# A routed attention and feed-forward kernel: when the first weight pieces are asked for and made up, and the order of factor stores and factor fetches

## The chip, the cores and the metric

The kernel runs on one core of one Trainium2 chip. Its time is the device time of one execution in microseconds. Three runs of the kernel before gave 940.28, 940.62 and 939.73, median 940.28. A profile is one more execution, taken by the hardware profiler: it took 940.7, of which the profile's span, from the first to the last instruction, is 938.8.

## The reference

Attention in which a query sees only the keys that were assigned to the same centroid, followed by a feed-forward block with the activation h - tanh(h). There are 4 batches, 8 heads, 768 positions of 64 elements, 16 centroids per head, and weights of 512 x 2048 and 2048 x 512 that come as 64-bit floats.

```python
q_assign = np.argmax(np.einsum('bhsd,hcd->bhsc', q_n, c_n), axis=-1)
k_assign = np.argmax(np.einsum('bhsd,hcd->bhsc', k_n, c_n), axis=-1)
mask = q_assign[:, :, :, None] == k_assign[:, :, None, :]
scores = scale * np.matmul(q, k.transpose(0, 1, 3, 2))
scores = np.where(mask, scores, -1000000000.0)
...
attn = attn / (np.sum(attn, axis=-1, keepdims=True) + 1e-09)
attn_out = np.matmul(attn, v)
...
h = x @ w_in
g = h - np.tanh(h)
return (g @ w_out)
```

## The kernel before

**Pairs, halves, steps.** Two heads are handled together, so there are 16 pairs, four to a batch. A pair's queries come in two halves of 384. The list `steps` holds (pair, half, s): each step takes two blocks of 128 keys (`s` is 0, 1 or 2) against one half of queries. Steps 0 to 11 are the first halves of the pairs of batch 0, 12 to 23 their second halves; from step 24 on a pair runs both halves in a row. `HALF` is 12. The loop over steps emits the program of all engines in a fixed order, written out by hand: nothing is moved by a scheduler afterwards, so an instruction waits behind whatever was emitted before it on its engine.

**One step.** `begin` of the next step computes scores on TensorE (L508, with a mask by one-hot codes added at L519 for pairs 1 to 3 of the first halves) and the exponential on ScalarE (L530). `value` multiplies the weights of this step with `vals` (L565). Where the mask is not in the scores, VectorE masks the weights with the codes of the queries, spread over all partitions in a tile `row` (`select`, L540). The tile pool for scores has two buffers, so the scores of one step want the exponentials of the step before.

**Codes.** The assigned centroid of each position is its code. `route` and `route_on` find it, `publish` (L439 to L443) puts the codes into `listed_codes` as a VectorE copy, transposes them and stores them to HBM in the tensor `q_codes`; `spread` (`row`) and `spread_both` (`hot`) read them back so that each partition has them all. `turn` makes the transposed tiles of queries and keys; for the first pairs it does so on TensorE, and copies the result out of PSUM on the engine that it is given (L369), or half and half on two engines if it is given none (L371, L372). `turn(0, 1, None)` stands in `centroid_norms`.

**Weight pieces.** The weights arrive as 32 pieces of 512 KB, 64-bit words that must be made into 32-bit ones. `fetch(at)` asks for a piece from POOL's queue (L218) into one of three buffers `raw`; `rest_of` makes a partial result on ScalarE (L150, L151) into one of two buffers `rest`; `round_piece` finishes it on VectorE (L159, L162) and fetches the piece three further on. The dictionary `paces` says how many pieces are made up in each of the steps 0 to 20. The first three fetches stand in the prologue, each behind a gate: `held_back(x)` is a POOL copy of one column that waits until `x` is there (L1304).

**Factors.** The later batches multiply with a scheme that needs seven combinations of quarters of each weight matrix instead of eight products of quarters. `up_maker` and `down_maker` compute the combinations on VectorE (`made`, L848; up to three live at a time) and store them, and the plain quarters that are needed as they are, to HBM (L831, from SP's queue); `maker` makes the list of such items. The items of `down_maker` are emitted in the steps 36 and 38 to 41, with a share of the list in each. From there the tiles are streamed: `fetch_factors` (L871) and `fetch_extra` (L1017) load them into the freed quarters of `w_in`. `EXTRAS_AT` says in which steps the first three extra factors (products 6, 7 and 4 of the half batch that is still open) are fetched. All SP loads and stores leave from one queue, in the order of emission.

Of the kernel before, what the change touches and what calls it, by code (L numbers as in the profile page):

```python
# [58 lines left out]
def kernel(  # L59
# [10 lines left out]
    nc = tc.nc  # L70
# [12 lines left out]
    TB = S // 2  # L83
# [25 lines left out]
    listed_codes = const.tile([P, 32], BF16, name="listed_codes")  # L109
# [70 lines left out]
    def fast():  # L180
# [29 lines left out]
        def fetch(at: int):  # L210
            if at >= len(PIECES):
                return
            dst, src = PIECES[at]
            if words == 1:
                nc.gpsimd.dma_start(dst, src)
                return
            raws[at] = rawp.tile([P, 2 * FQ * P], U32, name="raw")
            nc.gpsimd.dma_start(raws[at], src)  # L218
# [30 lines left out]
        def late_constants():  # L249
            nc.vector.tensor_scalar_mul(out=cn, in0=cen, scalar1=rden)  # L250
            spread_ = const.tile([P, 2, D], F32, name="spread_")
            nc.vector.memset(spread_, 0.0)
            nc.vector.tensor_copy(
                out=spread_[:, :, 0:C], in_=down.unsqueeze(1).to_broadcast([P, 2, C])
            )
            spread_ = spread_.rearrange("p a c -> p (a c)")
            nc.vector.tensor_tensor(out=spread_, in0=spread_, in1=ident, op=ALU.mult)
            nc.vector.reduce_sum(out=mine_code, in_=spread_, axis=AX.X)
# [9 lines left out]
        def centroid_norms():  # L268


            sq = const.tile([P, D], F32, name="sq")
            ss = const.tile([P, 1], F32, name="ss")
            nc.vector.tensor_tensor(out=sq, in0=cen, in1=cen, op=ALU.mult)
            nc.vector.reduce_sum(out=ss, in_=sq, axis=AX.X)
            nrm = const.tile([P, 1], F32, name="nrm")
            nc.scalar.sqrt(nrm, ss)

            nc.scalar.activation(out=sq[0:1, 0:1], in_=nrm[0:1], func=ACT.Exp)

            for it in range(2):  # L280
                lim = const.tile([P, 1], F32, name=f"lim{it}")
                nc.vector.tensor_scalar_max(lim, nrm, TINY)
                rec = const.tile([P, 1], F32, name=f"rec{it}")
                nc.vector.reciprocal(out=rec, in_=lim)
                two = const.tile([P, 1], F32, name=f"two{it}")
                nc.vector.scalar_tensor_tensor(
                    out=two, in0=ss, scalar=rec, in1=nrm, op0=ALU.mult, op1=ALU.add
                )
                nrm = const.tile([P, 1], F32, name=f"nrm{it}")
                nc.vector.tensor_scalar_mul(out=nrm, in0=two, scalar1=0.5)  # L290
            den = const.tile([P, 1], F32, name="den")
            nc.vector.tensor_scalar_add(den, nrm, 1e-6)
            nc.vector.reciprocal(out=rden, in_=den)
            both = const.tile([P, 2, D], F32, name="both")
            nc.vector.scalar_tensor_tensor(
                out=both, in0=cen.unsqueeze(1).to_broadcast([P, 2, D]), scalar=rden,
                in1=mines.unsqueeze(2).to_broadcast([P, 2, D]), op0=ALU.mult, op1=ALU.mult,
            )
            turn(0, 0, nc.scalar)
            pc = ps_a.tile([P, P], F32, name="pc", tag="a")  # L300
            nc.tensor.transpose(out=pc, in_=both.rearrange("p a d -> p (a d)"), identity=ident)
            nc.vector.tensor_copy(out=bd.rearrange("p a c -> p (a c)"), in_=pc)
            turn(0, 1, None)

        def keep_warm(times: int):

# [42 lines left out]
        def turn(n: int, i: int, engine):  # L349

            if not rowwise(n):
                x = raw_qk.pop((n, i))
                pool = turnp0 if n in (2, 3) else turnp
                t = turned[n, i] = pool.tile([P, 2, TB], F32, name=f"t{i}")
                nc.vector.transpose(
                    out=t.rearrange("p a n -> p (a n)"), in_=x.rearrange("p b d -> p (b d)")
                )
                return
            pt = ps_s.tile([P, 2, 512], F32, name="pt", tag="s")
            x = raw_qk.pop((n, i))  # L360
            for j in range(NCH):
                nc.tensor.transpose(
                    out=pt[:, j // HCH, (j % HCH) * P : (j % HCH + 1) * P],
                    in_=x[:, j].rearrange("p h d -> p (h d)"), identity=ident,
                )
            pool = turnp0 if n in (2, 3) else turnp
            t = turned[n, i] = pool.tile([P, 2, TB], F32, name=f"t{i}")
            if engine is nc.scalar:
                nc.scalar.copy(out=t, in_=pt[:, :, 0:TB])  # L369
                return  # L370
            nc.scalar.copy(out=t[:, 0], in_=pt[:, 0, 0:TB])  # L371
            nc.vector.tensor_copy(out=t[:, 1], in_=pt[:, 1, 0:TB])  # L372

        sims = {}

# [57 lines left out]
        def publish(n: int):  # L433

            sides = 2 if masked(n, 0) else 1
            G = HCH * 4 * sides
            code = codes[n] if sides == 2 else codes[n][:, 0]
            code = code.rearrange("p a b c -> p (a b c)" if sides == 2 else "p j h -> p (j h)")
            nc.vector.tensor_copy(out=listed_codes[:, 0:G], in_=code)  # L439
            t = rtp.tile([P, BL], BF16, name="qc")  # L440
            nc.vector.transpose(out=t, in_=listed_codes)
            kept = dram.tile([BL, P], BF16, name="q_codes")
            nc.sync.dma_start(kept.rearrange("c (g t) -> g c t", t=BL), t)  # L443
            if sides == 1:
                q_codes[n] = kept[0:G].rearrange("(a j h) p -> a j h p", a=2, h=2)
            else:
                q_codes[n] = kept[0:G].rearrange("(h i a j) p -> h i a j p", h=2, i=sides, a=2)

        rows, hots = {}, {}
# [392 lines left out]
        def maker(quarters, their, sums_, keep, shape, last=False):  # L842
            made = {}

            def make(which, x, y, op):
                x, y = (made[i] if isinstance(i, int) else i for i in (x, y))
                t = made[which] = rawp.tile(shape, F32, name="made", tag="raw")
                nc.vector.tensor_tensor(out=t, in0=x, in1=y, op=op)  # L848

            items, plain = [], [lambda i=i: keep(their[i], quarters[i]) for i in range(len(quarters))]  # L850
            for i, args in enumerate(sums_):
                items.append(lambda args=args: make(*args))
                if i < len(quarters) and not last:
                    items.append(plain[i])
                items.append(lambda args=args: keep(args[0], made[args[0]]))
            return items + plain if last else items

        streams = {}
        PER = HF + len(PRODUCTS)
# [154 lines left out]
        def fetch_extra(e: int):  # L1014
            t = w_in[(0, 2, 1)[(HF + e) % 3]].rearrange("p c f -> p (c f)")[:, 0 : HF * HM]
            extras[e] = t.rearrange("p (a b) -> p a b", b=HM)
            nc.sync.dma_start(extras[e], down_factors[SLOT[EXTRAS[e]]])  # L1017
# [183 lines left out]
        HALF = HP * NS  # L1201
# [101 lines left out]
        def held_back(x):  # L1303
            nc.gpsimd.tensor_copy(out=gate, in_=x)  # L1304
# [9 lines left out]
        turn(1, 0, nc.scalar)  # L1314
        turn(1, 1, nc.scalar)
        publish(0)
        late_constants()
        spread(0, 0)
        held_back(rows[0, 0][:, 0, 0, 0:1])
        fetch(0)  # L1320
        similar(1)
        turn_back(1)
        begin(steps[1])
# [22 lines left out]

        EXTRAS_AT = (3 * HALF + 4, 3 * HALF + 6, 3 * HALF + 7)
        paces = dict(enumerate((0, 1, 0, 1, 1, 0, 2, 2, 2, 1, 1, 0, 3, 3, 2, 2, 2, 2, 2, 3, 2)))  # L1350
        late, divides, makers, later, listed = [], [], [], {}, []
        begun, selected = set(), set()
        fill, whole, spent, since, over = [], 0.0, 0.0, 0, 1
        for at, (n, half, s) in enumerate(steps):
# [7 lines left out]
            if at == 2 * HALF - 4:  # L1362
                makers = [it for i in range(2) for it in up_maker(i)]
            if at == 2 * HALF:
                makers = [it for i in range(2) for it in down_maker(i)]
            now = []
            part = (at - since + 1) / over
            while fill and (spent + fill[0][0] / 2 <= whole * part or part == 1):
# [87 lines left out]
            todo = []  # L1456
# [34 lines left out]
            light = [i for i in range(max(at, 3 * HALF), 3 * HALF + 6) if i % 6 != 1]  # L1491
            if at < 2 * HALF - 1:
                light = list(range(at, 2 * HALF - 1))
            if makers and at in light:
                share = -(-len(makers) // len(light))
                if at == 2 * HALF - 2:
                    todo += [lambda n=n: fetch_factors(n - HF) for n in range(2)]
                todo += makers[:share]
                del makers[:share]
            if at in EXTRAS_AT:  # L1500
                todo.append(lambda e=EXTRAS_AT.index(at): fetch_extra(e))
            if "raw" in late_pools:
                todo += [check_done, check_done, check_on, check_on]
                if p == HP - 1 and half == 1 and s == NS - 2:
# [260 lines left out]
```

## Time and profile before

| what | us |
|---|---|
| median of three runs | 940.28 |
| the profiled execution | 940.7 |
| its span | 938.8 |
| VectorE's masks, L540 | 184.9 in 336 instructions |
| ScalarE's exponentials, L530 | 125.9 in 168 |
| loads of weight pieces, 32 of 512 KB, from issue to landing (median) | 4.7 to 4.8 |

The granted TensorE clock was 0.998 over the span. In the timeline each row gives the start, the duration, the engine, the line and operation, what it writes and reads, how many like it were merged, and in brackets how long the engine was idle before and what ended that. PE is TensorE, PEld its weight load, DVE VectorE, ACT ScalarE, POOL GpSimd and SPq the queue of SyncE. A busy TensorE is modelled as back to back matmuls, so a hole is visible only where nothing was running.

### The profile page before, as it was taken

What the parts mean: (1) busy time and instruction counts of PE and PEld (TensorE: products, weight loads), DVE (VectorE), ACT (ScalarE), POOL (GpSimd) and SP (SyncE); (2) the same over time, 40 slices, a digit from 0 to 9 for tenths busy, and PEclk for the clock granted to TensorE, in tenths of its full rate; (3) what the DMA queues carried; (4) which work ended last, traced back from release to release, by engine and by line L of the source; (5) the groups of instructions that cost most, each with busy time, mean ns of one, the idle gap of its engine ahead of it and who ended that gap; (6) DMA issues with size and microseconds to landing.
All of it is one profiled execution on the core that took longest, in us unless ns stands there. A gap on an engine that the chain in (4) does not pass through costs nothing.

```text
span 938.8 us, 17135 instructions
## 1 busy us (share of the span) xinstructions
PE 927.4 (99%) x6646; PEld 470.1 (50%) x6646; DVE 597.6 (64%) x1132; ACT 293.3 (31%) x454; POOL 528.4 (56%) x396
## 2 busy tenths in 40 slices
PE   8999999999999999999999999999999999999997
PEld 5434443355653454444466664444466665445665
DVE  7568676887789688576756578666855347443011
ACT  5686554234332232332321121333231310221000
POOL 0126343467778576776884354777796443657500
PEclk9999999999999999999999999999999999999999
DMA  7685455894527986475664647455434322323331
GB/s 169 198 233 156 147 142 134 233 284 128 132 69 210 286 254 153 136 160 163 191 162 162 154 147 214 131 181 153 147 90 150 99 85 102 118 87 128 108 107 38
DMA packets 169033, 144.13 MB, mean 154 GB/s; under 512 B 118336, under 2 KB 146800, under 8 KB 165744
## 3 DMA queue, kind: packets, MB, share of 16 engines
q1 hardware_dynamic: 159248, 119.72, 45.6%
q0 software_dynamic: 6240, 21.50, 7.0%
q10 hardware_dynamic: 3456, 1.74, 0.6%
q8 instruction: 55, 0.90, 0.4%
q14 instruction: 34, 0.28, 0.1%
HBM read 121.68 MB, written 21.24 MB: 152 GB/s over the span
## 4 chain that ended last, share of the span: by engine, by line
PE 90%; DMA 3%; DVE 3%; POOL 1%; ACT 1%; issue 1%; SPq 0%; DVEq 0%; POOLq 0%; ACTq 0%
PE pu L940 26%; PE pd L1148 23%; PE sc L508 13%; PE av L565 12%; PE o L755 6%; PE hd L1049 3%; PE h L739 2%; PE sim L384 1%; DMA hot<-q_codes 1%; DVE e L540 1%; PE den L626 1%; DMA den<-back 1%; DVE w_in L162 1%; POOL sum L556 1%; PE den L599 1%
## 5 line engine op out<-in xcount | busy, mean ns | idle before, releaser
L556 POOL TENSOR_TENSOR sum<-sum,e 128x768 f32<-128x768 f32 x112 | 206.1, 1840 | 87.4 <-DVE e L540 83.0
L540 DVE SCALAR_TENSOR_TENSOR e<-row,code,sc 128x384 f32<-128x384 bf16 x336 | 184.9, 607 | 75.3 <-ACT sc L530 49.3
L1148 PE MATMUL pd<-w_in,G 128*64 128x256 f32 (+1 forms) x1728 | 191.6, 379 | 0.0
L530 ACT ACTIVATE sc<-sc 128x768 f32<-128x768 f32 x168 | 125.9, 790 | 193.2 <-PE sc L508 156.1
L1148 PEld LDWEIGHTS pd<-w_in,G 128*64 128x64 f32 (+1 forms) x1728 | 130.5, 144 | 61.7 <-issue 5.9
L940 PE MATMUL pu<-xT,w_in 128*64 128x384 f32 (+1 forms) x1024 | 158.7, 447 | 0.6 <-PE pu L940 0.4
L508 PE MATMUL sc<-t,t 64*128 64x384 f32 x768 | 149.6, 507 | 1.6 <-ACT e L530 1.2
L565 PE MATMUL av<-e,vals 128*64 128x384 f32 x768 | 144.3, 498 | 0.0
L1112 POOL TENSOR_TENSOR G<-G,th 128x768 f32<-128x768 f32 (+1 forms) x51 | 87.1, 1724 | 67.7 <-ACT th L1110 67.5
L940 PEld LDWEIGHTS pu<-xT,w_in 128*64 128x64 f32 x1024 | 73.2, 137 | 74.2 <-issue 60.6
L508 PEld LDWEIGHTS sc<-t,t 64*128 64x128 f32 x768 | 66.5, 186 | 73.4 <-issue 34.5
L940 PE MATMUL pu<-diff,w_in 128*64 128x384 f32 x576 | 101.6, 487 | 0.0
L552 POOL TENSOR_TENSOR sum<-e 128x768 f32<-128x768 f32 x28 | 51.9, 1852 | 66.7 <-DVE e L540 63.1
L565 PEld LDWEIGHTS av<-e,vals 128*64 128x64 f32 x768 | 47.5, 136 | 81.1 <-issue 78.9
L1110 ACT ACTIVATE th<-G 128x768 f32<-128x768 f32 (+1 forms) x51 | 40.9, 806 | 148.9 <-DVE G L935 148.6
L940 PEld LDWEIGHTS pu<-diff,w_in 128*64 128x64 f32 x576 | 40.9, 137 | 51.7 <-issue 45.6
L755 PE MATMUL o<-w_out,g 128*64 128x512 f32 x256 | 57.4, 593 | 0.0
L935 DVE TENSOR_TENSOR G<-pu,u 128x384 f32<-128x384 f32 x72 | 39.6, 550 | 27.1 <-PE pu L940 27.1
L1165 DVE SCALAR_TENSOR_TENSOR c<-pd,w_in 128x256 f32<-128x256 f32 x36 | 15.1, 419 | 49.1 <-PE pd L1148 49.1
L739 PE MATMUL h<-xT,w_in 128*64 128x384 f32 x256 | 42.9, 487 | 0.3 <-DVE g L746 0.3
L1165 DVE SCALAR_TENSOR_TENSOR w_in<-pd,w_in 128x256 f32<-128x256 f32 x31 | 13.0, 419 | 45.5 <-PE pd L1148 44.9
L935 DVE TENSOR_TENSOR u<-pu,u 128x384 f32<-128x384 f32 x48 | 26.5, 551 | 15.8 <-PE pu L940 15.7
(160 smaller groups left out, 927.5 us busy)
## 6 DMA issues: line engine op xcount, KB each, us to landing
w_in<-up_factors SPq DMA_DIRECT2D x32, 896.0 KB
w_in<-down_factors SPq DMA_DIRECT2D x25, 1024.0 KB
raw<-in_moe_w_in_dram POOLq DMA_DIRECT2D x16, 512.0 KB, 4.8
raw<-in_moe_w_out_dram POOLq DMA_DIRECT2D x16, 512.0 KB, 4.7
again<-in_moe_w_in_dram SPq DMA_DIRECT2D x32, 256.0 KB
again<-in_moe_w_out_dram SPq DMA_DIRECT2D x32, 256.0 KB
vals<-in_v_dram SPq DMA_DIRECT2D x32, 192.0 KB
row<-q_codes SPq DMA_DIRECT2D x29, 192.0 KB
```

Source lines behind the costliest of these rows:

```text
L508: nc.tensor.matmul(sc[i][:, h, 0:TB], lhsT=turned[n, 1][r].rearrange("p a n -> p (a n)")[:, j * P : (j + 1) * P], rhs=turned[n, 0][r, half ...
L530: nc.scalar.activation(out=out, in_=sc[i][:, :, 0:TB], func=ACT.Exp, scale=SCALE)
L540: nc.vector.scalar_tensor_tensor(out=e[:, h].rearrange("p (j n) -> p j n", n=P), in0=rows[n, half][:, h], scalar=(codes[n][:, h, 1, j : j ...
L552: nc.gpsimd.tensor_tensor(out=s, in0=pair[0], in1=pair[1], op=ALU.add)
L556: nc.gpsimd.tensor_tensor(out=s, in0=s, in1=pair[i], op=ALU.add)
L565: nc.tensor.matmul(avs[n, half][h * D : h * D + D], lhsT=vals[n][:, h, j], rhs=e[i][:, h], start=(j == 0), stop=(j == NCH - 1),)
L739: nc.tensor.matmul(h[r], lhsT=w_in[i][:, c, o * P : (o + 1) * P][:, r], rhs=xT[c][:, half], start=(c == 0), stop=(c == CD - 1),)
L755: nc.tensor.matmul(acc[sub][r], lhsT=gs[f % HF][:, f // HF, sub * P : (sub + 1) * P][:, r], rhs=w_out[f // FQ][:, f % FQ], start=(f == seq ...
L935: nc.vector.tensor_tensor(out=out, in0=x, in1=y, op=ALU.add)
L940: nc.tensor.matmul(ps[r], lhsT=streams[base + i][:, c, k_, r], rhs=right[c], start=(c == 0), stop=(c == CH - 1),)
L1112: nc.gpsimd.tensor_tensor(out=t, in0=t, in1=th, op=ALU.subtract)
L1148: nc.tensor.matmul(out_, lhsT=w, rhs=x, start=(i == 0), stop=(i == HF - 1))
```

## The change

There are four edits.

1. `turn(0, 1, None)` becomes `turn(0, 1, nc.scalar)`: ScalarE copies the whole tile. The branch for an engine other than ScalarE becomes one whole VectorE copy; no call reaches it.
2. In the prologue the gate and fetch of piece 0 move ahead of `late_constants` and `spread`, and the gate looks at `listed_codes` in place of the spread row.
3. `paces` has 1 in place of 0 for step 5 and 1 in place of 2 for step 7, so the pieces from the fourth on shift: one is made up in step 5, two in step 6, one in step 7.
4. `down_maker` gives the made items and the plain stores apart; the made items of both quarters are emitted first, then all plain stores. `EXTRAS_AT` has steps 40, 41 and 42 in place of 40, 42 and 43, and within a step the fetch is emitted ahead of the makers' items.

On the engines this moves the following. On SP the stores run: five made tiles, with the codes' store among them, in place of two made tiles and three plain stores; the first factor's fetch then stands ahead of the last made tile and of all plain stores, the second ahead of four plain stores, the third ahead of the row of codes and the loads of the next pair, in place of behind them. On VectorE two `made` instructions move ahead of the masks or codes that stood before them; one pair of finishing instructions (L159, L162) moves ahead of the `hot` work of pair 3 (L483, L487). On ScalarE a pair L150, L151 moves ahead of the copy L604 of step 5. TensorE's order does not change.

```diff
-            turn(0, 1, None)
+            turn(0, 1, nc.scalar)
...
             if engine is nc.scalar:
                 nc.scalar.copy(out=t, in_=pt[:, :, 0:TB])
-                return
-            nc.scalar.copy(out=t[:, 0], in_=pt[:, 0, 0:TB])
-            nc.vector.tensor_copy(out=t[:, 1], in_=pt[:, 1, 0:TB])
+            else:
+                nc.vector.tensor_copy(out=t, in_=pt[:, :, 0:TB])
...
-            return items + plain if last else items
+            return (items, plain) if last else items
...
         publish(0)
+        held_back(listed_codes[:, 0:1])
+        fetch(0)
         late_constants()
         spread(0, 0)
-        held_back(rows[0, 0][:, 0, 0, 0:1])
-        fetch(0)
...
-        EXTRAS_AT = (3 * HALF + 4, 3 * HALF + 6, 3 * HALF + 7)
-        paces = dict(enumerate((0, 1, 0, 1, 1, 0, 2, 2, 2, 1, 1, 0, 3, 3, 2, 2, 2, 2, 2, 3, 2)))
+        EXTRAS_AT = (3 * HALF + 4, 3 * HALF + 5, 3 * HALF + 6)
+        paces = dict(enumerate((0, 1, 0, 1, 1, 1, 2, 1, 2, 1, 1, 0, 3, 3, 2, 2, 2, 2, 2, 3, 2)))
...
             if at == 2 * HALF:
-                makers = [it for i in range(2) for it in down_maker(i)]
+                made_, plain_ = zip(*[down_maker(i) for i in range(2)])
+                makers = [it for part in made_ + plain_ for it in part]
...
+            if at in EXTRAS_AT:
+                todo.append(lambda e=EXTRAS_AT.index(at): fetch_extra(e))
             if makers and at in light:
...
-            if at in EXTRAS_AT:
-                todo.append(lambda e=EXTRAS_AT.index(at): fetch_extra(e))
```

## The prediction

> **What bounds the kernel now.** I read the busy line first, then the list of who waited for whom, then the timeline at each wait found. The page:
>
> ```profile
> PE 927.4 (99%) x6646; PEld 470.1 (50%) x6646; DVE 597.6 (64%) x1132; ACT 293.3 (31%) x454; POOL 528.4 (56%) x396
> ```
>
> TensorE has work for all but 11.4 us of the 938.8 us span. The table of busy time by stretch places them: 2.07 in 0 to 10 us, 1.08 in 10 to 20, 0.23 in 20 to 30, 0.15 in 30 to 40, 1.19 in 50 to 60, 0.12 and 0.13 in the next two, 0.27 in 90 to 100, 0.8 in all of 100 to 900, and 5.35 after 900, where the last stores drain. The change adds and removes no matmul, so it can only fill those holes or dig new ones. The list of waits names the ones that it can touch:
>
> ```profile
> PE sc L508 <- ACT e L530: 1.2, 1, 1.2
> PE sim L384 <- DVE t L372: 0.7, 1, 0.7
> PE sc L519 <- DVE hot L487: 0.2, 1, 0.2
> ```
>
> One wait each, one place each. That is the whole stake: 1.2 + 0.7 + 0.2 = 2.1 us, 0.23% of the run, and part of the middle one must stay.
>
> **Part 1, the copy of the second turned tile (`turn(0, 1, ...)`).**
>
> ```profile
> 7.83 0.48 ACT L371 COPY t<-pt 128x384 f32<-128x384 f32 x1 [0.60 <-PE pt L362]
> 8.34 0.56 DVE L372 COPY t<-pt 128x384 f32<-128x384 f32 x1 [1.35 <-ACT t L371]
> 8.95 0.53 PE L384 MATMUL sim<-t,bd 128*32 128x192 f32 x8 [0.70 <-DVE t L372]
> ```
>
> The two halves were meant for two engines at once, but VectorE's half starts when ScalarE's ends: they run in line, 7.83 to 8.90, and TensorE follows 0.05 later. The change lets ScalarE copy all 768 columns. The row for exactly that, the first turned tile (6.43, L369, 128x768), has 0.80. So the tile is whole at 7.83 + 0.80 = 8.63, TensorE starts at about 8.69: **-0.26**. What follows (L394 at 9.55, the exponentials at 10.38, the next transposes at 11.24) names TensorE or ScalarE as what it waited for, not a load, so all of it comes 0.26 earlier.
>
> **Part 2, the first weight piece.** `fetch(0)` hung on the spread codes (`row`), POOL's gate at 18.41 and the issue at 18.53; now it hangs on `listed_codes`, written at 12.56 + 0.17 = 12.73, less 0.26. POOL has nothing else to do there; gate at about 12.5, issue at about 12.65. On POOL only the second gate is behind it, which waits for `hot` anyway.
>
> What it frees: the 512 KB no longer travel beside the two `hot` loads (issued 19.76). These landed for VectorE at 25.62, and TensorE waited 0.23 at 26.33. Without the load beside them `hot` is there before VectorE has done its twelve masks (18.45 + 6.44 = 24.89), which then decide: 24.9 + 0.42 + 0.31 is under the 26.10 at which TensorE ends its matmuls (both less 0.26). **-0.23**.
>
> What it costs: it now travels beside the write of the first codes, which the spread waits for, and the masks for the spread. Three writes of codes in the timeline:
>
> ```profile
> 13.00 0.64 SPq L443 DMA_DIRECT2D q_codes<-qc  x1
> ...
> 15.07 0.34 SPq L463 DMA_DIRECT2D row<-q_codes  x1
> ...
> 30.69 0.56 SPq L443 DMA_DIRECT2D q_codes<-qc  x1
> ...
> 34.32 1.14 SPq L472 DMA_DIRECT2D hot<-q_codes  x2
> ```
>
> Alone, the read that hangs on the write is issued 2.07 later (13.00 to 15.07; also 17.77 to 19.76); with weight pieces in flight 3.63 later (30.69 to 34.32). So the two ends are 0 and +1.6. Slack there is small: masks start at 18.45 the moment the row is there, each pair of them takes 1.07, and TensorE wants the second pair at about 20.85, ready at 20.6. Once TensorE is 0.26 earlier there is none left, so every microsecond by which the row is late counts whole. [...] But it is only so if the piece is there first. In the packet records of this trace the write's first packet comes 1.24 after its issue (13.00 to 14.24) and the piece's 1.38 after its own (18.53 to 19.91): 12.74 + 1.24 = 13.98 against 12.65 + 1.38 = 14.03, and the write's packets need only 0.3. A photo finish, a little in favour of the codes; before 14.0 the third pair's loads occupy the engines in both kernels. I take **+0.35**, a quarter of the crowded price, and keep -0.2 and +1.6 for the range.
>
> **Part 3, the paces.** Step 5 now makes up one piece and step 7 one instead of two; the sum over the steps 0 to 8 stays 9. This is the largest hole:
>
> ```profile
> 48.49 0.53 POOL L218 DMA_DIRECT2D raw<-in_moe_w_in_dram  x1 [6.96 <-ACT rest L151]
> ...
> 54.84 0.80 ACT L150 ACTIVATE rest<-raw 128x512 uint16<-128x512 uint32 x1 [2.60 <-DMA raw<-in_moe_w_in_dram]
> ...
> 56.12 1.48 ACT L530 ACTIVATE e<-sc 128x768 f32<-128x768 f32 x2
> ...
> 56.95 0.30 PEld L508 LDWEIGHTS sc<-t,t 64*128 64x128 f32 x4 [1.88 <-ACT e L530]
> 56.95 1.61 PE L508 MATMUL sc<-t,t 64*128 64x384 f32 x8 [1.19 <-ACT e L530]
> ```
>
> ScalarE's second piece of step 7 waits 2.60 for its load, and step 9's exponential stands behind it in program order; its scores were ready at 53.54. Now: piece 3 goes to step 5, where ScalarE ends `xT` at 43.39 and the next exponential starts at 45.40 for want of scores. 1.42 for the piece (the like pair at 46.79 ends 48.20) and 0.49 for `den` end at 45.30: it fits by 0.1, and a miss would be covered, since TensorE needs that exponential's buffer only at 47.61. The piece's load landed at 33.9. VectorE then finishes it at about 45.5 and POOL asks for the next load at about 45.0 instead of 48.49, so the piece left in step 7 (at 50.83) finds its load landed: 45.0 + 6.3, the slow landing of the one issued at 48.49, is 51.3, and ScalarE has room to 53.5 less 1.4 = 52.1. The two pairs of `hot` work (50.08) keep their place, one finished piece ahead of them being now another one. The exponential starts at 53.5, its first half frees the buffer at 54.3, TensorE comes at 55.76: no wait. **-1.19**, and -0.05 for the matmuls stretched to 1.61 from 1.56: **-1.24**. What is late next: step 11's scores (61.84, then 60.6) want half of step 10's exponential, which has `den` and pieces 7 and 8 before it: 56.3 + 2.9 = 59.2, half done at 60.0, in time by 0.6. The wait of 0.27 at 99.00 hangs on a chain of VectorE and ScalarE work that starts from TensorE's own scores at 81.83, so it moves along and stays.
>
> **Part 4, the down factors.** The order on SP becomes: all the made tiles' stores, the fetch of each factor as soon as its step (40, 41, 42) comes, plain quarters' stores behind. TensorE's busy time in 275 to 350 is 75.00 of 75.00, and the products that use the fetched tiles start at 320.22, 326.6 and 336.6 with the fetches issued at 307.86, 317.00 and 328.69. No hole, so no gain: **0**. On VectorE one `made` (1.21 to 2.8) moves ahead of the masks of 298.22, whose first user is at 302.54; cover 2.2. The dearer side is under the rivals; bound +2.
>
> **Sum.** -0.26 - 0.23 + 0.35 - 1.24 + 0 = -1.38. The profiled execution took 940.7 (span 938.8 and 1.9 around it) and stands 0.4 over the median of 940.28; it becomes 939.3, the median **938.9**.
>
> **The rivals.**
>
> *More than the sum.* The codes win outright (-0.35 - 0.2) and one of the small waits goes too because loads run one piece ahead from 45 us on (0.27 at 99.00, the 0.1 to 0.3 around 70): -1.38 - 0.55 - 0.35 = -2.3, 938.0. For it: ScalarE waits 1.27 for a load at 96.24. Against it: that load's issue at 91.42 hung on VectorE, not on earlier loads. Chance 0.30.
>
> *The removed wait is replaced.* The crowded price at the codes (+1.25 over my value), or step 7's load is late by as much as before because it now travels beside step 8's `hot` and `vals` (issued 45.56 to 47.34): 1.2 of the gain goes, 940.1. For it: 3.63 against 2.07 above. Chance 0.15.
>
> *Slower: codes behind factors.* At 318.26 the row of codes was issued and VectorE could start on it at 326.17 only, after a wait of 2.71: the queue was full of stores and one factor. Now a second megabyte and one more plain store of 512 KB go ahead of it. The stretch moves about 390 GB/s, so 1.5 MB are 3.9 us if nothing before it drains earlier. The masks are wanted at 330.62; two of them are done 1.07 after the row. The cover is 330.62 - 327.24 = 3.4, less the 1.4 that TensorE is earlier: 2.0. At 3.9 the stall is 1.9 and the gain of 1.4 is more than gone; with the loads of `x` and the next row (338.38) pushed alike and a second stall of that size the run is 938.9 + 3.8 = 942.7. It is a loss from 3.4 us later on, and one that can be measured from 5.3 on. Against it: the first factor now goes some 5 us earlier into a queue that was half empty (303 to 306, 308 to 309 in the packet records), which pays about as much back. Chance of any loss 0.13.
>
> **Chances and range.** The forecast as worked out has 0.42, the others 0.30, 0.15, 0.13. 0.2% is 1.9 us and about what a measurement of this kernel tells from no change: the forecast and the second rival lie inside, the first rival mostly outside (some of it within, some of the forecast beyond), the last mostly over. Faster 0.33, same 0.54, slower 0.13. The forecast's own range is 938.3 to 939.8; with the first rival below and the second above: 937.9 to 940.5.
>
> **What would show it.** The second `sim` group at 8.69 without VectorE before it; POOL's first load at about 12.6 and the first row's issue at 14.8 (codes first) or past 16 (piece first); no wait for `hot` near 26; scores of step 10 at about 55.6 with no wait for ScalarE; ScalarE free before 53.5; no wait of TensorE between 275 and 350. Wrong if TensorE waits for masks near 20 or 330, or if the wait at 57 only moves.

## The result, and the profile after

The changed kernel takes **948.02 us** (median of six runs, 947.13 to 951.15) against 940.03 for the kernel before beside it (six runs, 939.56 to 943.22): ratio 1.0083, 95% interval 1.0063 to 1.0103. It is slower by 8 us, where 1.4 us of gain were forecast. The profiled execution took 948.67, its span is 946.9. In some executions of most of these kernels, the kernel before among them, the time is some 4 us longer (in three of the profiles below a read of `hot` lands late near 53), so medians and ratios over many runs are compared, and in a profile the single places.

The busy line of the page, and TensorE's rows from the list of who waited for whom (us in total, times, longest):

```profile
PE 930.5 (98%) x6646; PEld 470.9 (50%) x6646; DVE 598.3 (63%) x1131; ACT 293.3 (31%) x454; POOL 529.8 (56%) x396
```

```profile
PE sc L507 <- DVE e L539: 4.7, 2, 4.1
...
PE tally L710 <- ACT den L603: 0.7, 1, 0.7
PE av L564 <- DVE e L539: 0.7, 1, 0.7
```

Two things are to be seen. The wait of 1.2 for ScalarE's exponential and that of 0.2 for `hot` are gone, as forecast, and three of 0.7 or more that did not exist have come. And TensorE's busy time rose by 3.1 us though it runs the same 6646 instructions: some ran slower.

Since TensorE's order is the same, each of its instructions can be set against itself before. The difference in start time at the places where it changes:

| at (time in before) | after less before | what happened there |
|---|---|---|
| 8.95 | -0.41 | turn copy; 0.14 of it are loads that came earlier in this execution |
| 21.1 | +1.30 | first weighted values wait 0.70 for masks, whose four pairs then set their pace |
| 26.3 | +0.91 | no wait for `hot` |
| 56.95 | -0.36 | no wait for ScalarE: 1.27 won |
| 58.8 | +0.37 | the tally waits 0.72 |
| 61.8 | +0.56 | small waits |
| 69.8 | +1.08 | scores wait 0.59 for masks |
| 302 | +1.22 | |
| 329.1 | +5.40 | scores wait 4.13 for masks |
| 332.0 | +8.04 | the 16 matmuls since then, scores and values, take nearly twice as long |
| end | +8.05 | |

So 6.8 of the 8.05 us lie at one place, near 330, and they come in two parts: a wait (4.2) and a slow stretch behind it (2.6). TensorE there, first in the timeline of before, then of after:

```profile
328.38 0.82 PE L599 MATMUL den<-sum,ones 128*64 128x384 f32 x4
329.13 1.56 PE L508 MATMUL sc<-t,t 64*128 64x384 f32 x8
330.62 1.51 PE L565 MATMUL av<-e,vals 128*64 128x384 f32 x8
```

```profile
329.58 0.82 PE L598 MATMUL den<-sum,ones 128*64 128x384 f32 x4
334.53 2.93 PE L507 MATMUL sc<-t,t 64*128 64x384 f32 x8 [4.13 <-DVE e L539]
337.39 2.77 PE L564 MATMUL av<-e,vals 128*64 128x384 f32 x8
340.00 1.89 PE L1048 MATMUL hd<-w_in,g 128*64 128x256 f32 x16
```

The same scores take 2.93 in place of 1.56 and the same values 2.77 in place of 1.51. The table of busy time by stretch (start:end, length, then busy time of PE, PEld, DVE, ACT and POOL, the granted clock, DMA share, GB/s) names the reason:

```profile
330.00:335.00 5.00, 0.87 (x6) 0.50 (x4) 1.75 (x4) 0.49 (x1) 0.00 (x0) 0.82 0.93 114
335.00:340.00 5.00, 5.00 (x17) 1.72 (x15) 3.53 (x7) 1.59 (x2) 4.30 (x3) 0.50 0.94 231
```

TensorE hardly worked in the first five microseconds and was granted half its clock in the next. The clock records of the trace have the half clock from 333.15 for 6.83 us.

What the masks waited for is read backward. On VectorE, first before, then after:

```profile
323.24 0.22 DVE L666 RECIPROCAL each<-each 128x12 f32<-128x12 f32 x1
326.17 2.19 DVE L540 SCALAR_TENSOR_TENSOR e<-row,code,sc 128x384 f32<-128x384 bf16 x4 [2.71 <-DMA row<-q_codes]
```

```profile
329.19 0.23 DVE L665 RECIPROCAL each<-each 128x12 f32<-128x12 f32 x1 [4.67 <-DMA each<-list]
333.25 2.19 DVE L539 SCALAR_TENSOR_TENSOR e<-row,code,sc 128x384 f32<-128x384 bf16 x4 [3.82 <-DMA row<-q_codes]
```

VectorE stands in line twice: for `each`, a small read of the denominators, which in before was there without a wait, and then for the row of codes. SyncE's queue shows why, first before, then after:

```profile
313.21 2.19 SPq L831 DMA_DIRECT2D down_factors<-w_out  x3
315.56 1.40 SPq L650 DMA_DIRECT2D each<-list  x1
317.00 1.21 SPq L1017 DMA_DIRECT2D w_in<-down_factors  x1
318.26 0.45 SPq L463 DMA_DIRECT2D row<-q_codes  x1
```

```profile
313.81 0.35 SPq L1016 DMA_DIRECT2D w_in<-down_factors  x1
314.26 3.96 SPq L830 DMA_DIRECT2D down_factors<-w_out  x4
318.33 3.18 SPq L649 DMA_DIRECT2D each<-list  x1
321.56 1.02 SPq L1016 DMA_DIRECT2D w_in<-down_factors  x1
322.62 0.77 SPq L462 DMA_DIRECT2D row<-q_codes  x1
```

Four plain stores in place of three go out ahead of `each`, and so does the second factor's megabyte (the first row), which in before stood behind it (317.00). The third factor's megabyte, which before went out at 328.69, now stands between `each` and the row. The row is issued 4.4 us later, and its masks start 10.6 after the issue in place of 7.9, with more in flight ahead of it.

### The profile page after: what moved, and what is told of

Its sections match the earlier page's. It is cut to its first block, busy times and chain, and to the rows that moved or that the text cites. A ratio compares the mean times of both kernels' runs of the same rounds, so it can differ in the third digit from the quotient of the medians.

```text
span 946.9 us, 17134 instructions
## 1 busy us (share of the span) xinstructions
PE 930.5 (98%) x6646; PEld 470.9 (50%) x6646; DVE 598.3 (63%) x1131; ACT 293.3 (31%) x454; POOL 529.8 (56%) x396
## 4 chain that ended last, share of the span: by engine, by line
PE 88%; DMA 4%; DVE 3%; POOL 2%; ACT 1%; SPq 1%; issue 1%; DVEq 0%; ACTq 0%; POOLq 0%
PE pu L939 26%; PE pd L1147 23%; PE sc L507 13%; PE av L564 13%; PE o L754 6%; PE h L738 2%; PE hd L1048 2%; DMA row<-q_codes 1%; PE sim L383 1%; DVE e L539 1%; PE den L625 1%; POOL sum L555 1%; DVE w_in L162 1%; PE den L579 1%; PE den L598 1%
## 5 line engine op out<-in xcount | busy, mean ns | idle before, releaser
L564 PE MATMUL av<-e,vals 128*64 128x384 f32 x768 | 146.5, 501 | 0.7 <-DVE e L539 0.7
```

The costliest lines, as they stand in the source:

```text
L564: nc.tensor.matmul(avs[n, half][h * D : h * D + D], lhsT=vals[n][:, h, j], rhs=e[i][:, h], start=(j == 0), stop=(j == NCH - 1),)
```

## The experiments

Each of these has the kernel before beside it on the same chip; that one's median was 940.04, 939.72 and 940.92 in the three sets.

### Without the factors' edit

In the changed kernel, the edit is taken back:

```diff
-                made_, plain_ = zip(*[down_maker(i) for i in range(2)])
-                makers = [it for part in made_ + plain_ for it in part]
+                makers = [it for i in range(2) for it in down_maker(i)]
...
-EXTRAS_AT = (3 * HALF + 4, 3 * HALF + 5, 3 * HALF + 6)
+EXTRAS_AT = (3 * HALF + 4, 3 * HALF + 6, 3 * HALF + 7)
```

The fetch goes back behind the makers' items within its step, too.

> The changed kernel without its fourth edit (order of factor stores and fetches as before). Queue theory: the row of codes near 318 us lands in time again, TensorE has no wait between 275 and 350 and no half clock; what is left is the first part of the kernel, 1.2 us later than before: 941.2 (940.7 to 941.7). Rival, that the late start of the first part shifts the loads and makes the row late by itself: a wait of 2 us or more for masks near 330 and 943 or more.

941.95, ratio 1.0015 (0.9999 to 1.0032). Between 320 and 345 TensorE is busy for 25.00 of 25.00, at full clock. So the rival is out. Of the 8 us, 6 are gone with this edit. By the medians 1.9 stay with the other three, a little over the expected range, but the interval still allows no change; in the profile TensorE ends 0.4 later than in before.

### The factors' edit alone

The other three edits are taken back: the copy of the turned tile, the gate of the first piece and the paces are those of the kernel before.

```diff
-turn(0, 1, nc.scalar)
+turn(0, 1, None)
...
-held_back(listed_codes[:, 0:1])
-fetch(0)
 late_constants()
 spread(0, 0)
+held_back(rows[0, 0][:, 0, 0, 0:1])
+fetch(0)
...
-paces = dict(enumerate((0, 1, 0, 1, 1, 1, 2, 1, 2, 1, ...)))
+paces = dict(enumerate((0, 1, 0, 1, 1, 0, 2, 2, 2, 1, ...)))
```

> The kernel before with the fourth edit alone. Queue theory: a wait of about 4 us near 330 and a stretch of half clock behind it, 6.8 us in all: 946.8 (945.5 to 947.5). Rival, that the lateness comes from both edits together: under 943.

946.45, ratio 1.0050 (1.0025 to 1.0075): 6.4 us over before. The profile has the wait (3.37 for the scores, half clock from 336.13 for 3.41 us). The factors' edit is the main cause, by itself.

### The third fetch one step later

In the changed kernel:

```diff
-EXTRAS_AT = (3 * HALF + 4, 3 * HALF + 5, 3 * HALF + 6)
+EXTRAS_AT = (3 * HALF + 4, 3 * HALF + 5, 3 * HALF + 7)
```

> The changed kernel with the third extra factor fetched in step 43 as before, behind the row of codes and the loads of the next pair, the rest of the fourth edit kept. If the third factor's megabyte ahead of the row is what makes it late: VectorE starts on that row 2.6 us or more earlier than 333.25, the wait of TensorE falls from 4.1 to under 1.5, no half clock, 941.5 to 943. If the four plain stores of 512 KB ahead of it are: the wait stays over 3 and the time over 946.

943.20, ratio 1.0030 (1.0017 to 1.0042): 4.8 us under the changed kernel by one fetch put behind the row of codes. VectorE in this run:

```profile
332.27 0.23 DVE L666 RECIPROCAL each<-each 128x12 f32<-128x12 f32 x1 [4.60 <-DMA each<-list]
332.69 2.19 DVE L540 SCALAR_TENSOR_TENSOR e<-row,code,sc 128x384 f32<-128x384 bf16 x4 [0.20 <-DMA row<-q_codes]
```

The wait for the row is 0.20 in place of 3.82. That for `each` is as long as it was: this part belongs to what still goes out ahead of it, the four plain stores and the second factor's fetch. Counted from TensorE's own lateness before this place, the masks start 2.2 us late here and 5.9 in the changed kernel. So the third fetch is 3.7 of it, and the stores and the second fetch are 2.2. TensorE waits 0.44 at the first scores and there is no half clock at this place.

### The order of stores alone

In the kernel before:

```diff
+made_, plain_ = zip(*[down_maker(i) for i in range(2)])
+makers = [it for part in made_ + plain_ for it in part]
-makers = [it for i in range(2) for it in down_maker(i)]
```

> The kernel before with the made stores first and the plain stores behind them, fetches in their old steps. If the megabyte decides: the row lands within 1.5 us of its old time, no wait, 940.0. If the plain stores decide: a wait of TensorE near 330 of 2 us or more, 943 or more.

942.58, ratio 1.0019 (1.0005 to 1.0034). Neither expectation is met. The list of waits shows a third mechanism:

```profile
PE hd L1049 <- DMA w_in<-down_factors: 1.2, 1, 1.2
```

With the four plain stores ahead of it the second factor's fetch is issued at 320.34 in place of 317.00, and TensorE, which multiplies with that factor at 326.7, waits for it. By the medians the order alone costs 2.5 us; in its profile TensorE falls back 1.4 at this wait. In the whole change, where the second factor is fetched earlier, this wait is not there, and that for the row of codes is. This run also splits the wait for `each`. Here the second fetch stands behind it, and VectorE waits 2.15 for it; where the fetch stands ahead of it, it waits 4.67 (the changed kernel) and 4.60 (third fetch later):

```profile
325.47 0.23 DVE L666 RECIPROCAL each<-each 128x12 f32<-128x12 f32 x1 [2.15 <-DMA each<-list]
```

The earlier fetches without the new order of stores were not tried, so what they cost by themselves stays open.

### TensorE kept busy during the wait

Two runs put matmuls without use ahead of the scores that wait. The first, in the changed kernel, wrote to an accumulator that was not free:

```diff
+if at == 3 * HALF + 9:
+    keep_warm(8)
 begin(following)
```

> The changed kernel with eight matmuls of 128x256 without use [...] ahead of the scores that waited 4.13 us near 330; they fill most of that wait. If the half clock that followed the wait came from TensorE standing idle, it stays at full clock there and the run is 2.0 to 2.6 us under the changed kernel (945.4 to 946). If the clock fell for another reason [...], the run is as long as the changed kernel (948) or longer.

951.44, ratio 1.0128 (1.0113 to 1.0144). A miss of the experiment: the added matmuls waited 4.74 us for that accumulator, which VectorE frees behind the late masks, and so came behind the wait (334.60, 5.11 us) and not into it. The second took the accumulator of the weighted values, which ScalarE has read out by 327.7 in this run:

```diff
+if at == 3 * HALF + 9:
+    ps = ps_a.tile([P, P], F32, name="warm", tag="a")
+    for _ in range(16):
+        nc.tensor.matmul(ps, lhsT=ident, rhs=ident, start=True, stop=True)
 begin(following)
```

> The changed kernel with sixteen matmuls of 128x128 without use [...] put where its scores wait 4.13 us near 330, on the accumulator that is free there since 326, so that they run in the wait and not behind it. If the half clock comes from a stretch [...] in which TensorE hardly works, there is none near 333 and the run is 2.0 to 2.6 us under the changed kernel (945.4 to 946.0). If it has another cause, 948 or more.

945.99, ratio 1.0042 (1.0027 to 1.0057): 2.0 us under the changed kernel by the medians, with more work in it. TensorE in this run:

```profile
331.23 3.84 PE L1409 MATMUL warm<-ident 128*128 128x128 f32 x32
335.36 1.97 PE L508 MATMUL sc<-t,t 64*128 64x384 f32 x8 [0.29 <-DVE e L540]
337.26 1.51 PE L565 MATMUL av<-e,vals 128*64 128x384 f32 x8
```

The masks are as late as in the changed kernel (VectorE starts them at 334.17, 5.9 late by the same count), the values take 1.51 again, and no half clock is recorded before the end of the run. TensorE stands for 0.29 us ahead of these scores in place of 4.13, and the half clock of 6.83 us is gone: it came from TensorE standing idle, and it is the second part of the price. Of that part's 2.6 us it is some 2.2 (an estimate): the scores take 1.97 here at full clock as well, 0.41 over the 1.56 of before, because they wait for the second accumulator too.

### The first piece alone, and behind the codes

In the kernel before:

```diff
 publish(0)
+held_back(listed_codes[:, 0:1])
+fetch(0)
 late_constants()
 spread(0, 0)
-held_back(rows[0, 0][:, 0, 0, 0:1])
-fetch(0)
```

> The kernel before with the first piece asked for with the first codes, nothing else. The forecast's terms: +0.35 - 0.23 = 0.1 over before. My theory: the piece is there before the codes, the row of codes lands 1.3 us later, TensorE waits about 1.2 more near 20 and gets 0.2 back near 26; part of what is left is taken up by the wait of 1.19 near 57, which hangs on a load: 0.3 to 1.0 us over before. Rival: the lateness stays whole, 1.0 or more.

941.46, ratio 1.0017 (1.0006 to 1.0028): 1.7 us over before, so the rival that the lateness stays whole. TensorE waits 1.06 for masks near 20, and the wait near 57 shrinks by 0.4 only. The place in the changed kernel: SyncE, then POOL, then VectorE.

```profile
12.59 0.64 SPq L442 DMA_DIRECT2D q_codes<-qc  x1
16.64 0.35 SPq L462 DMA_DIRECT2D row<-q_codes  x1
```

```profile
12.50 0.69 POOL L218 DMA_DIRECT2D raw<-in_moe_w_in_dram  x1
```

```profile
19.79 6.44 DVE L539 SCALAR_TENSOR_TENSOR e<-row,code,e 128x384 f32<-128x384 bf16 x12 [2.38 <-DMA row<-q_codes]
```

The read that hangs on the codes' write is issued 4.05 after it, against 2.07 in before. In the packet records the piece's 4 KB packets run from 13.89 to 16.17 and the codes' from 15.00 to 16.13; in before the codes ran from 14.24 to 14.53. The piece was there first.

To see whether it is the order or the company that costs, the piece was put a little later, behind the codes, in the kernel of the run above:

```diff
 publish(0)
-held_back(listed_codes[:, 0:1])
+for _ in range(12):
+    held_back(listed_codes[:, 0:1])
 fetch(0)
```

> The kernel before with the first piece hung on the first codes as in the change, but with twelve copies of POOL in place of one ahead of it (0.1 to 0.18 us each), which put the piece's issue 1.3 to 2 us later, behind the codes' write. If the order of the two at the DMA engines is what cost the 1.7 us of the first piece alone, the codes' write has its packets within 1.6 us of its issue again, the row lands as in the kernel before, TensorE doesn't wait near 20, and the run is at before or 0.2 under it. If the piece costs as much by its mere company (the row's own read beside it), 1 us or more over before.

940.81, ratio 0.9993 (0.9979 to 1.0007): by the medians nothing is lost. SyncE and POOL in this run:

```profile
12.93 0.64 SPq L443 DMA_DIRECT2D q_codes<-qc  x1
14.99 0.35 SPq L463 DMA_DIRECT2D row<-q_codes  x1
```

```profile
12.72 3.01 POOL L1304 CAST gate<-listed_codes 128x1 f32<-128x1 bf16 x12 [11.40 <-DVE listed_codes L439]
15.67 0.69 POOL L218 DMA_DIRECT2D raw<-in_moe_w_in_dram  x1
```

The twelve copies took 3.0 us, more than the 1.3 to 2 expected. The codes are back at 2.06, TensorE waits for no masks near 20, and the piece's packets, from 17.07 on, meet only the last 0.7 us of the row's own read (15.98 to 17.73), so company beside that read is hardly tested. What makes TensorE wait near 20 is that the piece's packets come ahead of the codes' (13.89 against 15.00 in the changed kernel). That the earlier piece is free of cost otherwise isn't shown: the medians are the same, but the lower quartile of the runs, 940.6 against 940.0 in the kernel before beside it, is 0.6 over. Of the piece alone that quartile was 1.1 over.

### Turn copy and paces, and a third buffer

In the kernel before:

```diff
-turn(0, 1, None)
+turn(0, 1, nc.scalar)
-paces = dict(enumerate((0, 1, 0, 1, 1, 0, 2, 2, 2, 1, ...)))
+paces = dict(enumerate((0, 1, 0, 1, 1, 1, 2, 1, 2, 1, ...)))
```

> The kernel before with the turn copy and the paces of the change alone; first piece and factors as before. The forecast's own terms: -0.26 and -1.24, so 1.5 us under the before of the same chip, with no wait of TensorE for ScalarE near 57 and none put in its place. My theory now, from the changed kernel's trace: the wait near 57 goes, but the tally near 58.8 then waits 0.4 to 0.7 for the denominators' copy and the scores near 70 wait 0.4 to 0.8 for masks, both of which hang on loads that do not come earlier: 0.2 to 0.5 us under before.

940.12, ratio 1.0003 (0.9992 to 1.0015). The 1.5 us are not there. In the profile TensorE is 2.1 ahead of before at 56.95 and gives it back: 0.75 at the tally, 0.2 at 61, 0.3 at 69, 0.4 at 98.6, 0.2 at 251. The tally's place in the changed kernel, TensorE, then ScalarE and VectorE:

```profile
56.59 1.56 PE L507 MATMUL sc<-t,t 64*128 64x384 f32 x8
57.98 0.49 PE L518 MATMUL sc<-hot 64*128 64x384 bf16 x4
59.19 0.86 PE L710 MATMUL tally<-den,firsts 64*64 64x384 f32 x4 [0.72 <-ACT den L603]
```

```profile
58.65 0.49 ACT L603 ACTIVATE den<-den 128x384 f32<-128x384 f32 x1 [2.25 <-DMA other<-list]
```

```profile
58.01 0.56 DVE L700 TENSOR_TENSOR xT<-xT,den 128x384 f32<-128x384 f32 x1 [4.17 <-DMA den<-back]
```

ScalarE's row names a load, `other`, as what ended its wait. But its source, TensorE's sums, was done at 56.6, and it starts 0.08 after VectorE's scaling (58.01 to 58.57) ends. The copy writes a tile `den`, of which there are two, and the older one is read by that scaling, which itself waited for a load. If so, a third buffer takes the wait away:

```diff
+denp = cx.enter_context(tc.tile_pool(name="denp", bufs=3))
-t = dens[n, half] = sump.tile([P, TB], F32, name="den")
+t = dens[n, half] = denp.tile([P, TB], F32, name="den")
...
-t = dens[n, 0] = sump.tile([P, TB], F32, name="den")
+t = dens[n, 0] = denp.tile([P, TB], F32, name="den")
```

> Turn copy and paces of the change, and in addition three buffers in place of two for the denominators, so that the copy of the tally near 58 need not wait for an earlier scaling to free one. If that buffer is what holds the tally, its wait of 0.4 to 0.7 us near 58.8 goes; the scores near 70 then wait by as much more, since their masks hang on a load: 0 to 0.5 us under the same kernel with two buffers. If the wait stays, the buffer was not it.

938.90, ratio 0.9987 (0.9976 to 0.9998): 0.8 us under the kernel before by the medians, narrowly clear of noise, and 1.2 us under the same kernel with two buffers. TensorE, ScalarE and VectorE in this run:

```profile
55.31 1.56 PE L509 MATMUL sc<-t,t 64*128 64x384 f32 x8
56.70 0.49 PE L520 MATMUL sc<-hot 64*128 64x384 bf16 x4
57.13 0.86 PE L712 MATMUL tally<-den,firsts 64*64 64x384 f32 x4
```

```profile
55.45 0.49 ACT L605 ACTIVATE den<-den 128x384 f32<-128x384 f32 x1 [0.32 <-PE den L581]
```

```profile
56.71 0.73 DVE L702 TENSOR_TENSOR xT<-xT,den 128x384 f32<-128x384 f32 x1 [4.18 <-DMA den<-back]
```

The scaling waits as long as ever (4.18), and nobody waits for it: ScalarE's copy starts 1.3 us before the scaling does. My expectation that the scores near 70 would take the wait over was wrong; nothing is given back there, and TensorE keeps the 1.2 us that it wins near 56 to the end.

The same lines in the kernel before, with nothing else:

> The kernel before with the third buffer for the denominators and nothing else. My theory: no wait of TensorE hung on that buffer in the kernel before, it only held back what the paces had won; so no change against before within 0.3 us. Rival: the third buffer is what gained 0.8, and the paces gave nothing: 0.8 under before.

941.15, ratio 1.0001 (0.9985 to 1.0018). No gain of the third buffer by itself is seen, though the interval would allow one of up to 1.4 us. Its profile says the same: nothing changes near 58, where the kernel before has no wait for the tally. So the gain is that of the paces, and it needs the buffer to be kept.

And all together: the edits of the run with the third buffer, and the first piece behind the codes by twelve copies.

> Turn copy, paces, third buffer for the denominators, and the first piece behind the codes. If the parts add: 0.8 under before for the first three, as measured, and another 0.2 for the wait near 26: 1.0 us under before, 938.7. If the earlier piece crowds something else, 0.8 or less under before.

939.89, ratio 0.9986 (0.9965 to 1.0007). The profile is the shortest of all (span 937.1), with TensorE 1.9 ahead at the end, but the runs do not tell it from the kernel before, nor from the one without the moved piece. The version that beats both kernels is that with turn copy, paces and third buffer, by one set of runs.

## Why the prediction was wrong

**Part 4 is the step that failed.** It put the factors at "0" with "bound +2", and priced the mechanism that happened as its rival "codes behind factors", at 942.7 with a chance of 0.13. The runs give 6 us for this edit. Three terms were wrong.

- The cover. "The cover is 330.62 - 327.24 = 3.4" took the weighted values for the first that want the masks. The scores ahead of them want them too: the masks read the scores' two accumulators, and the next scores at 329.13 need one back. In after they start 1.28 behind the masks' start. By that, 326.17 + 1.28 = 327.45, and the cover was 1.7. The changed kernel (masks 5.9 late, 4.2 lost at the start of the scores), the factors alone (5.1, 3.4) and the third fetch later (2.2, 0.5) all leave 1.7.
- The lateness. 3.9 was taken for 1.5 MB; it is 5.9. The rate of "about 390 GB/s" was too high: while the row was under way, 318.26 to 326.17, the queues moved 277 in before, by which 1.5 MB are 5.4 us (an estimate). And `each` was left out: it stands ahead of the masks on VectorE, and is itself late behind four plain stores and the second factor's megabyte. No run shows that the first factor's earlier start, which was to "pay about as much back", paid anything.
- The clock, for which there was no term at all. 2.6 us of the loss come after the wait has ended, some 2.2 of them by the half clock.

**Part 2** named the right mechanism and sized it wrongly: +0.35, "a quarter of the crowded price", for a photo finish. TensorE fell back 1.7 us here in the changed kernel (from -0.40 to +1.30) and 2.1 with the piece alone, over the bound of +1.6. The issues were as forecast, 12.50 for the piece and 12.59 for the codes. By the times taken from before, the codes' first packet was to come at 12.59 + 1.24 = 13.83 and the piece's at 12.50 + 1.38 = 13.88. The piece's came at 13.89, the codes' at 15.00: a tie in these times was lost whole. The codes' last packet (16.13) came with the piece's last (16.17). The read that hangs on the codes was issued 4.05 after them in place of 2.07, 1.98 later, where the forecast, an estimate, had 1.6 at most. How the two queues share the engines isn't shown: these records do not name their engine. The gain at `hot`, -0.23, can't be put down to the move: TensorE won 0.39 between 21.1 and 26.3 in the changed kernel, but just as much in the order of stores alone (from +0.13 to -0.26), where the piece stood as before.

**Part 3** removed the wait near 57 as forecast (-1.27 against -1.24, by its own steps on ScalarE). It failed in "what is late next": it tested step 11's scores and the exponential, and not the tally between them, which needs a tile that a late load holds. The gain was lost behind that buffer: with three of them it stays.

**Part 1** was right: the tile is copied in 0.80 and TensorE starts its second `sim` group at 8.54, 0.41 earlier, of which the loads of that execution are 0.14, so 0.27 are left against 0.26.

## What to carry to other kernels

Where a transfer is put ahead of others in a queue, ask for each of those behind it who waits for it first: the cover ends at the earliest consumer, and an accumulator that has to be given back is one. When a wait goes, follow the tiles as well as the engines: the next limit may be a buffer whose last reader waits for a load, and one more buffer then decides whether the gain is kept. And a stall of TensorE can cost more than its length: here one of 4.13 us was followed by 6.83 us of half clock, one of 3.37 and one of 2.02 by 3.41 us each, and one of 1.78 by none. So it should be priced with the clock that follows.

## What the hardware showed that was not expected

The granted clock fell to half for 6.83 us in after and, at the places below, for 3.41 in two of the runs, and not from the start of the idle time: 2.75 us into it in after, 0.14 and 0.94 us behind its end in the two others. In after TensorE stood from 330.40 to 334.53 and the half clock ran from 333.15 to 339.98; the matmuls of the 5.45 us from 334.53 on took nearly twice as long. With the factors alone it stood from 332.62 to 335.99 and the half clock ran from 336.13 to 339.55; 1.6 us were lost. With the piece behind the codes it stood for 2.02 us only, from 52.81 to 54.84, for `hot`, and the half clock ran from 55.78 to 59.19.

In the table of busy time, first the 3.41 us ahead of the half clock and the two halves of it in after; then the 3.41 us ahead of the half clock with the piece behind the codes; last 3.41 us with a wait of 1.78 in them, behind which the clock stayed full (the order of stores alone):

```profile
329.74:333.15 3.41, 0.66 (x6) 0.00 (x0) 0.00 (x0) 0.49 (x1) 0.00 (x0) 1.00 0.95 101
333.15:336.57 3.42, 2.04 (x6) 1.22 (x8) 2.52 (x5) 0.30 (x1) 0.99 (x1) 0.50 0.98 147
336.57:339.98 3.41, 3.41 (x12) 1.00 (x10) 2.74 (x5) 1.29 (x2) 3.29 (x3) 0.50 0.92 275
```

```profile
52.37:55.78 3.41, 1.39 (x12) 0.54 (x10) 1.51 (x4) 1.11 (x2) 0.12 (x1) 1.00 0.90 309
```

```profile
55.05:58.46 3.41, 1.63 (x16) 0.67 (x10) 2.15 (x6) 3.29 (x6) 0.53 (x1) 1.00 0.61 213
```

TensorE worked 0.66 and 1.39 us in the stretches ahead of the half clock, and 1.63 in the one that none followed. How long TensorE has to stand for the clock to fall, and when it comes back, these traces don't show in general. They show the prices: stalls of 3.4 and 4.1 us cost 1.6 and 2.6 on top, and that of 1.78 us nothing.
